# An extra pair's rows of x gathered through DRAM instead of by one-hot products

## The chip, the cores and the metric

The kernel runs on one core of one Trainium2 chip. The metric is the device time of one execution in microseconds, median of three runs. All times in the profile are in microseconds from the start of the span unless marked ns.

## The reference

Attention with random features gives x (1152 tokens of 512). A first mixture-of-experts layer sends each token to the one of eight experts with the highest logit; a second layer sends every token through four experts. Only the first of these two matters here:

```python
e_idx = np.argmax(x @ w_gate, axis=1)
for e in range(E):
    mask = e_idx == e
    if not mask.any():
        continue
    h = np.maximum(x[mask] @ w1[e], 0.0)
    ye = h @ w2[e]
    out[mask] = gate_w[mask, None] * eom[mask, e, None] * ye
```

## The kernel before

Tokens lie in four chunks of 288 (two batches of 576). Each chunk is made of two main tiles of 128 rows and a rest of 32; the four rests share one tile. Each batch has a main expert, the one that most of its tokens choose, and a chunk goes through it whole: `unit1` is layer 1 (96 products into tiles `ph`, whose results ACT and DVE turn into `hh` and `hl`), `unit2_blocks` is layer 2 in four blocks of 24 products (tiles `py`), each multiplied by a row of gates (`gate_row`, tiles `dg`, `pg`, `gb`) and written to `x2T`. The products are done in split precision, three for each (lines 645 to 647).

Pairs of a chunk and another expert that some of its tokens chose are extras. `extras` (line 985) finds them on DVE from the counts. One of them is treated apart: the first pair, where it has at most 32 tokens (`SLOTS`). All other extras go through a loop behind a branch (`tc.If(nx > 0)`, line 1189) whose lists of experts and chunks (`le_t`, `lc_t`, and the selector `mt`) `extras` makes too, with passes over 128x1024 elements (lines 1027 to 1040).

The pair taken apart goes as follows. Its expert and chunk are read into registers from `wi_t` (lines 1056, 1057). SP loads the expert's layer-1 weights raw (`xw1`, line 1138 reads them) and then three tiles `xt` of the chunk's rows of x from the DRAM copy `xs` (lines 1062, 1063). `picked` makes a mask of its tokens, two products `pr` (lines 1079, 1080) count them, and DVE turns that into `rank`, each token's slot (lines 1082 to 1085). `og` is the one-hot matrix of the slots (line 1089), `ogf` the same times the gates. The products `px` (line 1109) of `og` and `xt` gather up to 32 rows for each of the three tiles; ACT copies them to `xpart`, four transposes and a DVE sum (`turned_sum`, lines 1104, 1105) give `xg`, the gathered columns. Layer 1 is `phx` (line 1138), copied, turned and summed into `hx`; layer 2 is `yx` (line 1149, with the weights `xw2` in `own`, `w2x` and two more tiles of the tag `xt`); `pyf` folds it, `pa` (line 1168) spreads it back, and DVE adds it to `x2T` (line 1173). E1, the main expert of the second batch, has its layer-1 weights loaded behind that (`E1.load1`, line 116, into the two buffers that `xw1` leaves) with the register read from `le_t`, and its layer-2 weights only behind the branch (line 143, called from `E1.load2`).

On each engine the order of instructions is set when the program is built: a planner with estimated durations takes, whenever an engine comes free, the earliest statement of the program that it holds to be ready. So a later statement may stand before an earlier one (`px` of line 1109 stands among the products of a `unit2` block that the program begins after it, and a memset of line 1177 runs before `extras`). On the chip each engine then follows this order strictly: an instruction that waits holds up everything behind it on its engine. `pin` and `tc.issue_after` force an order by hand.

Of the kernel before, what the change touches and what calls it, by code (L numbers as in the profile page):

```python
# [9 lines left out]
F32 = mybir.dt.float32  # L10
F32R = mybir.dt.float32r
I32 = mybir.dt.int32
AF = mybir.ActivationFunctionType
ALU = mybir.AluOpType
# [8 lines left out]
DM = 512  # L23
NE, NE2, FF = 8, 4, 1024
KB, FB = DM // 128, FF // 128
# [5 lines left out]
SLOTS = 32  # L31
# [7 lines left out]
def moe_stack(ctx, tc, q, k, v, omega, w_gate, w_ogate, mw1, mw2, dprobs, dw1, dw2, out):  # L39
    nc = tc.nc  # L40
    TT, STT, TS = nc.vector.tensor_tensor, nc.vector.scalar_tensor_tensor, nc.vector.tensor_scalar
# [120 lines left out]
    ap = pool_a.enter_context(tc.tile_pool(name="ap", bufs=2))  # L162
# [5 lines left out]
    for c, w, pattern, base in ((0, 32, [[1, 32]], 0), (32, 32, [[1, 32]], 1), (64, 8, [[-1, 8]], 8),  # L168
# [3 lines left out]
                       pattern=pattern, base=base, channel_multiplier=0)  # L172
# [45 lines left out]
    def load_v(b, hh):  # L218
        raw["v", b, hh] = load_main(v, b, hh, "v", G, D + 1)

    xs = ctx.enter_context(tc.tile_pool(name="dp", bufs=1, space=bass.MemoryType.DRAM)).tile([9, 128, DM], F32, name="xs")
    om2 = cp.tile([128, 2, D], F32, name="om2")
    for r in range(2):
        nc.scalar.dma_start(om2[:, r, :], omega)
# [34 lines left out]
    def pin(i):  # L259

        k = i.ins.engine
        if k in last_of:
            tc.add_manual_dep(i.ins, last_of[k].name,
                              mybir.DependencyInfo(mybir.DependencyClass.NoSync, mybir.DependencyReason.DATA))
        last_of[k] = i.ins
        return i
# [399 lines left out]
    E0, kv_step = None, {}  # L666
# [36 lines left out]
    while st < n:  # L703
# [72 lines left out]
        if gate_at == st - 1:  # L776
            gate_late[0] = (0, lg) + main_expert(0, mx, eq, ps_t, "pt")
            E0 = main_weights(0, nc.gpsimd)
# [101 lines left out]
    nd2 = Turn((ps_n, "nd"), (ps_m, "nm"))  # L880
# [46 lines left out]
    RINGS = ((ps_t, "pt"), ND)  # L927

    def unit1(c, w1, *rings):
        xhc = [xh[:, kb, NC * c:NC * c + NC] for kb in range(KB)]  # L930
        xlc = [xl[:, kb, NC * c:NC * c + NC] for kb in range(KB)]
        return l1(w1, xhc, xlc, *(rings or RINGS))

    def unit2_blocks(c, w2, hs, late=None):
        gb = gate_row(sel_static(c, c // 2))
        for d in range(KB):
            if d == KB - 1 and late is not None:
                late += [l2_block(w2, hs, d, (ps_k, "kv")), gb]
                yield
                return  # L940
            y = l2_block(w2, hs, d, (ps_k, "kv") if (c, d) == (0, 0) else None)
            for dst, src in zip(x2cols(c), (slice(0, 256), slice(256, NC))):
                TT(x2T[:, d, dst], y[:, src], gb[:, src], op=ALU.mult)
            yield
# [8 lines left out]
    def x2cols(c):  # L953
        return slice(256 * c, 256 * c + 256), slice(1024 + 32 * c, 1056 + 32 * c)
# [18 lines left out]
    hs = first  # L973
# [8 lines left out]
    x2T = yp.tile([128, KB, NX], F32, tag="y", name="x2T")  # L982


    def extras():
        fl = cp.tile([128, 4, NE], F32, name="fl")
        TS(fl, cnt, 0.5, None, op0=ALU.is_gt)
        nb = cp.tile([128, 2, NE], F32, name="nb")
        TS(nb, ohb, -1.0, 1.0, op0=ALU.mult, op1=ALU.add)
        for c in range(4):  # L990
            TT(fl[:, c], fl[:, c], nb[:, c // 2], op=ALU.mult)
        flat = fl.rearrange("p c e -> p (c e)")
        pa = cp.tile([128, 32], F32, name="pa")
        pb_ = cp.tile([128, 32], F32, name="pb_")
        src = flat
        for i, sft in enumerate((1, 2, 4, 8, 16)):
            dst = (pa, pb_)[i % 2]
            nc.vector.tensor_copy(dst[:, 0:sft], src[:, 0:sft])
            TT(dst[:, sft:32], src[:, sft:32], src[:, 0:32 - sft], op=ALU.add)
            src = dst  # L1000

        sel = cp.tile([128, 32], F32, name="sel1")
        STT(sel, src, 1.0, flat, op0=ALU.is_equal, op1=ALU.mult)
        sc = cp.tile([128, 32], F32, name="sc")
        TT(sc, sel, cnt.rearrange("p c e -> p (c e)"), op=ALU.mult)
        few = cp.tile([128, 2], F32, name="few")
        nc.vector.tensor_reduce(few[:, 0:1], sc, axis=AX.X, op=ALU.add)
        TS(few[:, 0:1], few[:, 0:1], SLOTS + 0.5, None, op0=ALU.is_lt)
        TS(few[:, 1:2], src[:, 31:32], 0.5, None, op0=ALU.is_gt)
        TT(few[:, 0:1], few[:, 0:1], few[:, 1:2], op=ALU.mult)  # L1010
        TS(sel, sel, few[:, 0:1], None, op0=ALU.mult)
        TT(flat, flat, sel, op=ALU.subtract)
        TS(src, src, few[:, 0:1], None, op0=ALU.subtract)
        where = cp.tile([128, 2], F32, name="where")
        for i, tab in enumerate((ue, uc)):
            TT(sc, sel, tab.rearrange("p c e -> p (c e)"), op=ALU.mult)
            nc.vector.tensor_reduce(where[:, i:i + 1], sc, axis=AX.X, op=ALU.add)
        wi = cp.tile([128, 2], I32, name="wi")
        nc.vector.tensor_copy(wi, where)
        nx = cp.tile([128, 1], I32, name="nx")  # L1020
        nc.vector.tensor_copy(nx, src[:, 31:32])
        mine = cp.tile([128, 32], F32, name="mine")
        TS(mine, iota, src[:, 31:32], None, op0=ALU.is_equal)
        TT(src, src, flat, op=ALU.mult)
        mt = lp.tile([128, 32, 4, NE], F32, name="mt", bufs=1)
        mv = mt.rearrange("p i c e -> p i (c e)")
        TT(mv, src.unsqueeze(1).to_broadcast([128, 32, 32]), iota1.unsqueeze(2).to_broadcast([128, 32, 32]),
           op=ALU.is_equal)
        lists = []
        pool_t = ExitStack()  # L1030
        ltp = pool_t.enter_context(tc.tile_pool(name="ltp", bufs=1))
        for nm, tab in (("le", ue), ("lc", uc)):
            t = ltp.tile([128, 32, 32], F32, tag="lt", name="lt")
            TT(t, mv, tab.rearrange("p c e -> p (c e)").unsqueeze(1).to_broadcast([128, 32, 32]), op=ALU.mult)
            s = cp.tile([128, 32], F32, name=nm + "f")
            nc.vector.tensor_reduce(s, t, axis=AX.X, op=ALU.add)
            if nm == "le":
                STT(s, mine, ef[1][:, 0:1], s, op0=ALU.mult, op1=ALU.add)
            si = cp.tile([128, 32], I32, name=nm)
            nc.vector.tensor_copy(si, s)  # L1040
            lists.append(si)
        pool_t.close()
        return nx, mt, lists[0], lists[1], sel.rearrange("p (c e) -> p c e", c=4), wi

    blocks = unit2_blocks(0, E0.w2, hs)
    next(blocks)
# [2 lines left out]
    gate_count(1, *ND)  # L1049
    for _ in blocks:  # L1050
        pass
    nx_t, mt, le_t, lc_t, sel1, wi_t = extras()
    hs = unit1(1, E0.w1)
    pool_x = ExitStack()
    xg_ = pool_x.enter_context(tc.tile_pool(name="xg", bufs=1))
    ex = nc.values_load(wi_t[0:1, 0:1], engines=[SP], min_val=0, max_val=NE - 1)
    cx = nc.values_load(wi_t[0:1, 1:2], engines=[SP, DVE], min_val=0, max_val=3)
    X = Expert(dyn(mw1, ex), dyn(mw2, ex))
    xw1 = X.raw1()
    xt = [xg_.tile([128, DM], F32, tag="xt", name="xt", bufs=3) for _ in range(3)]  # L1060
    for t in range(2):
        nc.sync.dma_start(xt[t], xs[bass.ds(cx * 2 + t, 1)].rearrange("o p d -> (o p) d"))
    nc.sync.dma_start(xt[2], xs[8])

    def picked(nm, main, rest):

# [10 lines left out]
    mask, fac = picked("mask", f32(oh_all), f32(ohr)), picked("fac", g_all, grm)  # L1077
# [3 lines left out]
    rank = xg_.tile([128, 2, 3], F32, name="rank")  # L1081
    nc.vector.tensor_copy(rank, pr)
    for t in (1, 2):
        for i in range(t):
            TT(rank[:, 0, t:t + 1], rank[:, 0, t:t + 1], rank[:, 1, i:i + 1], op=ALU.add)
    og = xg_.tile([128, 3, SLOTS], F32, name="og")
    ogf = xg_.tile([128, 3, 4, SLOTS], F32, name="ogf")
    for t in range(3):
# [10 lines left out]
    def turned_sum(dst, src, n, bank):  # L1099

        pool, tag = bank
        ps = pool.tile([128, 4, n], F32, tag=tag, name="pts")
        for i in range(4):
            nc.tensor.transpose(ps[:, i], src[:, 128 * i:128 * i + 128], ident[:n, :n])
        nc.vector.tensor_reduce(dst, ps.rearrange("p i (k s) -> p i s k", s=SLOTS), axis=AX.X, op=ALU.add)

    px = nd2.tile([128, DM], F32, tag="nd", name="px")
    for t in range(3):
        nc.tensor.matmul(px[SLOTS * t:SLOTS * t + SLOTS], og[:, t], xt[t], start=True, stop=True)
    part = xg_.tile([128, 2, DM], F32, tag="part", name="xpart", bufs=1)  # L1110
    nc.scalar.copy(part[0:96, 0], px[0:96])
    xg = xg_.tile([128, KB, SLOTS], F32, name="xg")
    turned_sum(xg, part[0:96, 0], 96, RINGS[0])
    psx = ps_t.tile([128, 3, 128], F32, tag="pt", name="psx")
    for t in range(3):
        nc.tensor.transpose(psx[:, t], ogf[:, t].rearrange("p a s -> p (a s)"), ident)
# [4 lines left out]
    E1 = Expert(dyn(mw1, e), None, nc.vector)  # L1121
    xw2 = X.raw2(0, own)
    xw2 = [xw2[:, f] for f in range(4)]
    w2x = xg_.tile([128, 2, DM], F32, name="w2x")
    nc.sync.dma_start(w2x, X.wb[512:768, :].rearrange("(f p) d -> p f d", p=128))
    xw2 += [w2x[:, 0], w2x[:, 1]]
    for f in (6, 7):
# [44 lines left out]
        for dst, src in ((bass.ds(cx * 256, 256), slice(0, 256)), (slice(1024, NX), slice(256, 384))):  # L1172
            TT(x2T[:, d, dst], x2T[:, d, dst], pa[:, src], op=ALU.add)

    last = []
    for cols in x2cols(1):
        pin(nc.gpsimd.memset(x2T[:, KB - 1, cols], 0.0))
    blocks = unit2_blocks(1, E0.w2, hs, last)
    next(blocks)
    next(blocks)  # L1180
    yf = second()
    next(blocks)
# [304 lines left out]
```

## Time and profile before

| | us |
|---|---|
| median of 3 runs | 573.14 (572.75 to 573.24) |
| the profiled execution | 573.32 |
| its span, first to last instruction | 571.3 |
| PE busy in the span | 563.3 |
| DVE / ACT / POOL busy | 395.4 / 251.1 / 264.0 |

The profiled execution lies 0.18 us above the median and 2.0 us above its own span. The stretch that the change touches lies between 98 us (`extras`) and 153 us (the first layer-2 block of the third chunk). Only PE's row starts are exact enough to be subtracted from each other: the products of a full chunk follow each other every 0.133 us (12.8 us for 96), whatever durations their rows show.

### The profile page before, as it was taken

To read this page: it belongs to the slowest core of one execution; us is meant where nothing else is said; L and a number is where in the kernel's file an instruction comes from. 1 tells how busy PE (TensorE), PEld (TensorE's weight loads), DVE (VectorE), ACT (ScalarE), POOL (GpSimd) and SP (SyncE) were. 2 spreads that over 40 slices of the span, in tenths; PEclk is the share of its full clock that TensorE was granted. 3 is DMA by queue.
4 is the path that set the end of the run, shared out by engine and by line. 5 is a ranking of instruction groups with operands and counts; after the bars stand their busy time and mean duration, and the time that the engine had idled before them with its cause. 6 is when DMAs were issued, how large, how long until landed. Compare 5 with 4: busy or idle time off the path is not lost.

```text
span 571.3 us, 11664 instructions
## 1 busy us (share of the span) xinstructions
PE 563.3 (99%) x4526; PEld 510.5 (89%) x4527; DVE 395.4 (69%) x865; ACT 251.1 (44%) x622; POOL 264.0 (46%) x318
## 2 busy tenths in 40 slices
PE   8999999999999999999999999999999999999997
PEld 7787899987999999889989999899998999989996
DVE  7877978946679886666676666766666666665664
ACT  5988844135634434444342443334433344343230
POOL 5996464000010227673663836638456375563210
PEclk9999999999999999999999999999999999999999
DMA  8861560483600400220220022022022002000004
GB/s 181 211 167 39 176 207 1 168 294 110 224 1 3 136 11 2 75 74 1 75 73 1 2 75 74 2 73 75 1 74 75 0 28 85 38 2 1 0 1 165
DMA packets 42473, 42.83 MB, mean 75 GB/s; under 512 B 14896, under 2 KB 31792, under 8 KB 42416
## 3 DMA queue, kind: packets, MB, share of 16 engines
q1 hardware_dynamic: 42128, 42.00, 23.7%
q8 instruction: 36, 0.59, 0.4%
q14 instruction: 21, 0.17, 0.1%
q10 hardware_dynamic: 288, 0.07, 0.1%
HBM read 37.34 MB, written 4.72 MB: 74 GB/s over the span
## 4 chain that ended last, share of the span: by engine, by line
PE 73%; DMA 1%; DVE 1%; issue 0%; ACT 0%; SPq 0%; ACTq 0%
PE po L646 11%; PE po L645 11%; PE po L647 11%; PE pp L647 10%; PE pp L646 10%; PE pp L645 10%; PE py L645 2%; PE py L647 1%; PE py L646 1%; DMA st<-in_moe_w_dram 1%; PE ph L646 1%; PE ph L647 1%; PE ph L645 1%; DVE wlo L105 1%; DVE hl L641 0%
## 5 line engine op out<-in xcount | busy, mean ns | idle before, releaser
L105 POOL TENSOR_TENSOR wlo<-st,whi 128x512 fp32r<-128x512 f32 x96 | 115.7, 1226 | 178.6 <-ACT whi L104 72.0
L104 ACT CAST whi<-st 128x512 fp32r<-128x512 f32 x116 | 65.6, 590 | 117.4 <-PE po L647 49.3
L646 PE MATMUL po<-wlo,hh 128*128 128x512 f32 x290 | 112.8, 389 | 0.0
L645 PE MATMUL po<-whi,hh 128*128 128x512 f32 x290 | 112.7, 389 | 0.0
L647 PE MATMUL po<-whi,hl 128*128 128x512 f32 x290 | 112.4, 388 | 0.0
L888 POOL TENSOR_TENSOR hl<-c,hh 128x320 fp32r<-128x320 f32 (+1 forms) x64 | 52.2, 816 | 84.6 <-ACT hh L887 69.2
L647 PE MATMUL pp<-xh,wlo 128*128 128x320 f32 (+1 forms) x256 | 75.8, 296 | 0.0
L646 PE MATMUL pp<-xl,whi 128*128 128x320 f32 (+1 forms) x256 | 75.7, 296 | 0.0
L645 PE MATMUL pp<-xh,whi 128*128 128x320 f32 (+1 forms) x256 | 75.6, 295 | 0.0
L1422 DVE SCALAR_TENSOR_TENSOR oa<-po,pb,oa 128x512 f32<-128x512 f32 x75 | 55.1, 747 | 29.1 <-PE po L647 29.1
L647 PEld LDWEIGHTS po<-whi,hl 128*128 128x128 f32 x290 | 54.5, 188 | 11.4
L645 PEld LDWEIGHTS po<-whi,hh 128*128 128x128 f32 x290 | 54.5, 188 | 10.4
L646 PEld LDWEIGHTS po<-wlo,hh 128*128 128x128 f32 x290 | 54.5, 188 | 10.1
L1422 DVE SCALAR_TENSOR_TENSOR ob<-po,pb,ob 128x512 f32<-128x512 f32 x59 | 44.2, 749 | 26.8 <-PE po L647 26.8
L1377 DVE TENSOR_TENSOR c<-u,pp 128x320 f32<-128x320 f32 (+1 forms) x96 | 43.3, 453 | 22.4 <-PE pp L647 21.9
L886 ACT ACTIVATE c<-c 128x320 f32<-128x320 f32 (+1 forms) x64 | 28.5, 445 | 50.7 <-DVE c L1377 50.0
L646 PEld LDWEIGHTS pp<-xl,whi 128*128 128x128 f32 x256 | 48.5, 190 | 1.2
L645 PEld LDWEIGHTS pp<-xh,whi 128*128 128x128 f32 x256 | 48.5, 190 | 1.2
L647 PEld LDWEIGHTS pp<-xh,wlo 128*128 128x128 f32 x256 | 48.5, 190 | 0.0
L641 DVE SCALAR_TENSOR_TENSOR hl<-c,hh 128x320 fp32r<-128x320 f32 (+1 forms) x64 | 44.4, 725 | 0.5 <-ACT hh L640 0.2
L351 ACT ACTIVATE e<-pj,nb 128x128 f32<-128x128 f32 x144 | 39.1, 388 | 6.1 <-DVE nb L342 5.9
L645 PE MATMUL ph<-xh,whi 128*128 128x288 f32 x128 | 38.3, 299 | 0.5 <-PEq L1189 0.4
(280 smaller groups left out, 1249.7 us busy)
## 6 DMA issues: line engine op xcount, KB each, us to landing
st<-in_moe_w_dram SPq DMA_DIRECT2D x36, 512.0 KB, 4.5
st<-in_moe_w_dram SPq DMA_DIRECT2D x8, 1024.0 KB, 6.8
q<-in_q_dram SPq DMA_DIRECT2D x4, 512.0 KB, 4.9
v<-in_v_dram SPq DMA_DIRECT2D x16, 128.0 KB, 5.0
xs<-xn SPq DMA_DIRECT2D x16, 128.0 KB, 3.0
k<-in_k_dram SPq DMA_DIRECT2D x3, 512.0 KB, 5.1
out_dram<-oa SPq DMA_DIRECT2D x5, 256.0 KB, 2.0
own<-in_moe_w_dram SPq DMA_DIRECT2D x1, 1024.0 KB, 7.6
```

Of the source, the lines that this page charges most:

```text
L104: p(heng.tensor_copy(hi, src) if heng else nc.scalar.copy(hi, src))
L105: p(eng.tensor_tensor(lo, src, f32(hi), op=ALU.subtract))
L351: pin(nc.scalar.activation(e[:, i], st_p[u][a][:, i], AF.Exp, bias=nb[:, a, i:i + 1]))
L641: return lambda: p(STT(hl, src, 0.0, f32(hh), op0=ALU.max, op1=ALU.subtract))
L645: p(nc.tensor.matmul(ps, sh_, mh, start=start, stop=False))
L646: p(nc.tensor.matmul(ps, sh_, ml, start=False, stop=False))
L647: p(nc.tensor.matmul(ps, sl_, mh, start=False, stop=stop))
L886: nc.scalar.activation(c, c, AF.Relu)
L888: nc.gpsimd.tensor_tensor(hl, c, f32(hh), op=ALU.subtract)
L1377: TT(c, u, p, op=op)
L1422: STT(oacc[T], po, pc, oacc[T], op0=ALU.mult, op1=ALU.add)
```

## The change

The three one-hot products `px` and the copy `xpart` go. In their place each tile's masked rows are sent by an indirect transfer from POOL into a DRAM tile `xz` of 32 rows at the index `ix` (the rank; an index of 4096 and more, which the bounds check leaves out, for rows that aren't masked). The three `xz` are zeroed before, and read back after, by plain transfers from POOL into `xr`, whose transposes and sum give `xg` as before. The mask, the ranks and the transfers come ahead of `unit1(1)` in the program, the lists of the loop (`lists_of`) after `xg`, the first block of `unit2(1)` ahead of the transposes, and the loads of `xt` ahead of those of `xw1`.

```diff
@@ -218,7 +218,9 @@
-    xs = ctx.enter_context(tc.tile_pool(name="dp", bufs=1, space=bass.MemoryType.DRAM)).tile([9, 128, DM], F32, name="xs")
+    dp = ctx.enter_context(tc.tile_pool(name="dp", bufs=1, space=bass.MemoryType.DRAM))
+    xs = dp.tile([9, 128, DM], F32, name="xs")
+    xz = [dp.tile([SLOTS, DM], F32, name=f"xz{t}") for t in range(3)]
@@ -1019,6 +1021,9 @@
         nc.vector.tensor_copy(nx, src[:, 31:32])
+        return nx, sel.rearrange("p (c e) -> p c e", c=4), wi, src, flat
+
+    def lists_of(src, flat):
         mine = cp.tile([128, 32], F32, name="mine")
@@ -1027,10 +1032,8 @@
-        pool_t = ExitStack()
-        ltp = pool_t.enter_context(tc.tile_pool(name="ltp", bufs=1))
         for nm, tab in (("le", ue), ("lc", uc)):
-            t = ltp.tile([128, 32, 32], F32, tag="lt", name="lt")
+            t = xg_.tile([128, 32, 32], F32, tag="part", name="lt", bufs=1)
@@ -1039,8 +1042,7 @@
-        pool_t.close()
-        return nx, mt, lists[0], lists[1], sel.rearrange("p (c e) -> p c e", c=4), wi
+        return mt, lists[0], lists[1]
@@ -1049,18 +1051,25 @@
-    nx_t, mt, le_t, lc_t, sel1, wi_t = extras()
-    hs = unit1(1, E0.w1)
+    nx_t, sel1, wi_t, src_t, flat_t = extras()
     pool_x = ExitStack()
     xg_ = pool_x.enter_context(tc.tile_pool(name="xg", bufs=1))
     ...
-    xw1 = X.raw1()
     xt = [xg_.tile([128, DM], F32, tag="xt", name="xt", bufs=3) for _ in range(3)]
     for t in range(2):
         nc.sync.dma_start(xt[t], xs[bass.ds(cx * 2 + t, 1)].rearrange("o p d -> (o p) d"))
     nc.sync.dma_start(xt[2], xs[8])
+    xw1 = X.raw1()
+    w2x = xg_.tile([128, 2, DM], F32, name="w2x")
+    nc.gpsimd.memset(w2x[0:SLOTS, 0], 0.0)
+    pi = xg_.tile([128, 1], I32, name="pi")
+    nc.gpsimd.iota(pi, pattern=[[0, 1]], base=4096, channel_multiplier=1)
+    pf = xg_.tile([128, 1], F32, name="pf")
+    nc.gpsimd.tensor_copy(pf, pi)
+    for t in range(3):
+        nc.gpsimd.dma_start(xz[t], w2x[0:SLOTS, 0])
@@ -1083,6 +1092,19 @@
+    place = xg_.tile([128, 3], F32, name="place")
+    far = pf.to_broadcast([128, 3])
+    TT(place, rank[:, 0], far, op=ALU.subtract)
+    TT(place, place, mask, op=ALU.mult)
+    ix = xg_.tile([128, 3], I32, name="ix")
+    TT(ix, place, far, op=ALU.add)
+    for t in range(3):
+        nc.gpsimd.indirect_dma_start(xz[t], bass.IndirectOffsetOnAxis(ap=ix[:, t:t + 1], axis=0), xt[t], None,
+                                     bounds_check=SLOTS - 1, oob_is_err=False)
+    xr = xg_.tile([128, DM], F32, tag="xt", name="xr", bufs=3)
+    for t in range(3):
+        nc.gpsimd.dma_start(xr[SLOTS * t:SLOTS * t + SLOTS], xz[t])
+    hs = unit1(1, E0.w1)
@@ -1104,13 +1126,14 @@
-    px = nd2.tile([128, DM], F32, tag="nd", name="px")
-    for t in range(3):
-        nc.tensor.matmul(px[SLOTS * t:SLOTS * t + SLOTS], og[:, t], xt[t], start=True, stop=True)
-    part = xg_.tile([128, 2, DM], F32, tag="part", name="xpart", bufs=1)
-    nc.scalar.copy(part[0:96, 0], px[0:96])
+    last = []
+    for cols in x2cols(1):
+        pin(nc.gpsimd.memset(x2T[:, KB - 1, cols], 0.0))
+    blocks = unit2_blocks(1, E0.w2, hs, last)
+    next(blocks)
     xg = xg_.tile([128, KB, SLOTS], F32, name="xg")
-    turned_sum(xg, part[0:96, 0], 96, RINGS[0])
+    turned_sum(xg, xr[0:96], 96, RINGS[0])
+    mt, le_t, lc_t = lists_of(src_t, flat_t)
@@ -1121,7 +1144,6 @@
-    w2x = xg_.tile([128, 2, DM], F32, name="w2x")
     nc.sync.dma_start(w2x, X.wb[512:768, :].rearrange("(f p) d -> p f d", p=128))
@@ -1172,11 +1194,6 @@
-    last = []
-    for cols in x2cols(1):
-        pin(nc.gpsimd.memset(x2T[:, KB - 1, cols], 0.0))
-    blocks = unit2_blocks(1, E0.w2, hs, last)
-    next(blocks)
     next(blocks)
     yf = second()
```

## Rows read from the trace of the kernel before

**Rows 1.** The page's first part: busy time (share of the span) and instructions of each engine.

```profile
PE 563.3 (99%) x4526; PEld 510.5 (89%) x4527; DVE 395.4 (69%) x865; ACT 251.1 (44%) x622; POOL 264.0 (46%) x318
```

**Rows 2.** Busy time of each engine in stretches around the change, granted clock, DMA.

```profile
core 0: us, PE busy (x) PEld busy (x) DVE busy (x) ACT busy (x) POOL busy (x), PEclk, DMA share, GB/s
104.00:117.00 13.00, 13.00 (x100) 13.00 (x99) 9.66 (x26) 3.21 (x8) 0.00 (x0) 1.00 0.75 258
117.00:122.00 5.00, 5.00 (x35) 3.49 (x38) 3.28 (x16) 1.15 (x3) 0.00 (x0) 1.00 0.88 309
...
138.00:141.00 3.00, 2.55 (x19) 2.35 (x19) 0.98 (x3) 1.90 (x7) 0.00 (x0) 1.00 0.54 139
```

**Rows 3.** PE in order of time: start, us, line, operation, tile.

```profile
103.67 0.29 PE L645 MATMUL ph<-xh,whi 128*128 128x288 f32 x1
...
116.47 0.28 PE L1079 MATMUL pr<-mask,upper 128*128 128x3 f32 x2
...
116.83 0.38 PE L645 MATMUL py<-hh,whi 128*128 128x288 f32 x1
117.05 0.29 PE L646 MATMUL py<-hl,whi 128*128 128x288 f32 x1
...
117.97 0.30 PE L647 MATMUL py<-hh,wlo 128*128 128x288 f32 x1
118.20 1.41 PE L1109 MATMUL px<-xt,og 128*32 128x512 f32 x6
119.53 0.40 PE L645 MATMUL py<-hh,whi 128*128 128x288 f32 x1
...
120.44 0.49 PE L1104 MATMUL pts<-ident,xpart 96*128 96x96 f32 x4
...
121.58 1.92 PE L1138 MATMUL phx<-st,xg 128*32 128x512 f32 x16
...
124.62 0.51 PE L922 MATMUL pg<-dg,ones 128*128 128x288 f32 x2
124.97 0.29 PE L647 MATMUL py<-hh,wlo 128*128 128x288 f32 x1
```

**Rows 4.** The chain that ended last, in order of time: start, us, what.

```profile
137.99 7.48 DMA st<-in_moe_w_dram
...
152.62 0.53 PE pg L922 x2
```

**Rows 5.** DVE in order of time.

```profile
103.19 1.22 DVE L1027 TENSOR_TENSOR mt<-pa,consts 128x1024 f32<-128x1024 f32 x1
...
104.76 0.16 DVE L1019 CAST wi<-where 128x2 int32<-128x2 f32 x1
...
109.19 0.17 DVE L1040 CAST le<-lef 128x32 int32<-128x32 f32 x1
...
131.97 2.50 DVE L105 TENSOR_TENSOR wlo<-st,whi 128x512 fp32r<-128x512 f32 x4 [0.36 <-ACT whi L104]
134.70 0.52 DVE L943 TENSOR_TENSOR x2T<-py,gb 128x256 f32<-128x256 f32 x2 [0.23 <-PE py L647]
135.59 2.20 DVE L1173 TENSOR_TENSOR x2T<-x2T,pa 128x256 f32 x8 [0.37 <-issue]
```

**Rows 6.** SP's transfers in order of time: start, us of issue, line.

```profile
106.31 1.04 SPq L138 DMA_DIRECT2D st<-in_moe_w_dram  x2
110.97 0.93 SPq L1062 DMA_DIRECT2D xt<-xs  x2
...
122.71 1.24 SPq L116 DMA_DIRECT2D st<-in_moe_w_dram  x2
```

**Rows 7.** Transfers: line, engine, count, KB each, us to landing.

```profile
xt<-xs SPq DMA_DIRECT2D x3, 256.0 KB, 5.3
...
xs<-xn SPq DMA_DIRECT2D x4, 64.0 KB, 2.2
```

**Rows 8.** POOL in order of time.

```profile
156.34 2.73 POOL L105 TENSOR_TENSOR wlo<-st,whi 128x512 fp32r<-128x512 f32 x2 [64.23 <-PE py L647]
```

## The prediction

> **What bounds the kernel now.** I read the page's busy shares first: PE is busy for 563.3 of 571.3 us [rows 1], so a change counts for what it takes from PE's queue or makes PE wait. Then the stretches: from 104 to 122 us PE is busy throughout, at the full granted clock [rows 2], so there is no idle PE time to win there, only work to remove. Then PE in order of time. The 96 products of `unit1(1)` begin at 103.67 and end where `pr` begins, at 116.47: 12.8 us, 0.133 each. In the `unit2` block behind it stands `px`: after the product at 117.97 the next was due at 118.10 and comes at 119.53, so `px` costs PE 1.43 us [rows 3]. Last I read the chain that ended last. It doesn't follow PE here: it goes through the transfer of E1's layer-2 weights, issued at 137.99, and from there through ACT and DVE to PE at 152.62 [rows 4]. The transfer goes out when DVE has passed the branch, which it does after the eight additions of `pa` (135.59 for 2.20, so 137.79) [rows 5]. PE itself idles for 0.45 us around the branch [rows 2]. So two paths run level into 152 us, and a gain counts only as far as both move: PE's queue, and DVE's additions with the transfer behind them.
>
> **What the change removes.** `px`: 1.43 us of PE. ACT's copy of `px` goes too, but its place between 119.53 and the transposes at 120.44 was filled with `py` products [rows 3], so it is worth nothing.
>
> **What it moves on PE.** `pr` now falls among the products of `unit1(1)` and no longer at a border. A product after another kind of work is followed after 0.22 instead of 0.13 us (116.83 to 117.05) [rows 3], so the move costs 0.09. `pg` (0.35, from 124.62 to 124.97) stands before or inside the first block instead of later: nothing. Transposes, `phx`, `yx`, `pa` stay. Sum for PE: -1.43 + 0.09 = -1.34 us, if it never waits.
>
> **When PE wants `xr`.** The first block comes ahead of the transposes now. It ends at 103.67 + 12.8 + 0.36 for `pr` + 0.09 + 0.35 for `pg` + 24 x 0.133 + 0.09 = 120.5 us [rows 3]. There PE's queue is in fixed order: if `xr` isn't there, everything behind the transposes waits, `unit2` products included.
>
> **When `xr` comes.** `wi` was written at 104.76, behind the 1.22 us pass of `mt` [rows 5], which now comes later in the program; so about 103.5. From the end of `wi` (104.92) to SP's next transfer it was 1.39 us [rows 5, 6], so `xt` goes out from 104.9, three issues of 0.47 each (0.93 for two) [rows 6], the last at 105.8. Landing: 2.2 us for the 64 KB stores to `xs`, 5.3 for `xt` behind the 2 MB of `xw1` [rows 7]. The loads now go ahead of `xw1` on a quiet queue; I take 3.5: first at 108.4, last at 109.3. The ranks are no later: mask, `pr`, `rank` and the three operations for `place` and `ix` end by about 107, as their inputs are there by `wi` and small operations on DVE are of 0.16 us, as that of `wi` itself [rows 5].
>
> No row shows a transfer issued from POOL, nor an indirect one. For an issue I take bounds of 0.5 us (SP's, 0.52 for each of `xw1`) and 1.4 (the longest POOL work in these rows, 2.73 for two) [rows 6, 8], and 1.0 between. For a landing the bounds are again 2.2 and 5.3 [rows 7], and I take 3.0: the pieces are 64 KB or less, but the DMA engines are 75 to 88% busy from 104 to 122 us [rows 2]. Three indirect transfers are then issued by 108.4 + 3.0 = 111.4, landed at 114.4; the last read-back, issued by 115.4, lands at 118.4, 2.1 us ahead of 120.5. By the low bounds it is 104.9 + 2.2 + 3 x 0.5 + 2.2 + 0.5 + 2.2 = 113.5; by the high ones 104.9 + 5.3 + 3 x 1.4 + 5.3 + 1.4 + 5.3 = 126.4. So the slack is 2.1 us, within +7.0 and -5.9: hidden is likelier than not, and far from sure.
>
> The Trainium skill, page "DMA: Bandwidth & Descriptors", section "Anatomy of one DMA — SWDGE (gpsimd) path", gives a POOL transfer 2.0 us and its bytes at 436 GB/s, so an estimate of 2.15 us for 64 KB; two such landings in place of my two would have `xr` there at 116.7. No run here shows it yet.
>
> **What else moves.** The zeroing of `xz`, the memset, `pi` and `pf` are POOL's; POOL has nothing between its memsets of `x2T` and 156.34, 64.23 us of idle time [rows 8], and nothing queued behind the indirect transfers but the read-backs and the branch. On SP, `xw1` goes behind three `xt` issues (1.4 us) that start 1.4 us earlier: it goes out at 106.3 as before, and is first read at 121.58 [rows 3, 6]. `lists_of` stands after `xg` in the program, but its inputs are there from 103 us, and DVE is busy for only 9.66 of the 13 us from 104 to 117 with those passes in it [rows 2]; the planner takes what is ready, so I expect them where they were, `le` near 109 [rows 5], at no cost.
>
> **What DVE gives on.** The transposes come at 120.5 against 120.44, so `phx` and the two transfers of `E1.load1` that wait for it (122.71) stay where they are [rows 3, 6]. Then DVE's last four `wlo` (131.97 for 2.50), too, move little, at most by some 0.5 (an estimate) if ACT, which copies `ys` ahead of the casts for them, comes to that earlier. Behind them DVE has the last `x2T` product (0.52 at 134.70) and the additions [rows 5]. PE has `pa` ready 1.34 earlier, but DVE is free for the additions at about 134.0 to 134.5, plus 0.52: 134.5 to 135.0 against 135.59. So the second path gains 0.6 to 1.1 us, and the smaller of the two gains counts: I take 0.9.
>
> **Sum.** 573.32 - 0.9 = 572.4 for the profiled execution; it lies 0.18 above the median of the runs, so 572.2 for the median.
>
> **Rivals.** (1) *The gather comes late.* For it: six transfers on an engine that no row shows issuing any, two landings in DRAM in a row, beside the extra expert's weights. Each us after 120.5 costs PE one; from 121.8 the gain is gone, from about 122.7 the kernel is slower by over 0.2%. With both landings at 4.5, and 1.4 for each issue it is 104.9 + 3.5 + 4.2 + 4.5 + 1.4 + 4.5 = 123.0, and with `xt` at 5.3 124.8. With 124.2: 3.7 - 1.34 = 2.4 us slower, 575.5. A mechanism of this kind: POOL held up by DVE's long passes, 1.22 us each [rows 5], for its three indirect issues and the last read-back: 118.4 + 4 x 1.22 = 123.3. The Trainium skill, page "SBUF — State Buffer", sections "SBUF: two separate sides" and "Who interferes with whom", says that POOL can't write a transfer's descriptors while DVE runs in a two-port mode; but it names copies, casts and scalar operations for that, not products and sums. The casts here are of 0.16 and 0.17 us [rows 5], so I give this mechanism 0.03 of the rival's chance.
>
> (2) *The whole 1.34 comes through.* If DVE or ACT are put in another order (the additions ahead of the last `wlo`, or `ys` ahead of all of them), the second path moves as far as PE: 571.8.
>
> (3) *The lists aren't moved up*, so that the change does something else than it says. Then `le` is written three passes (3.7 us) and some 0.5 after `xg` (121.6), at 125.8; `E1.load1` goes out at 127.2 instead of 122.71, the last `wlo` end at 138.9 in place of 134.5, and the additions with the transfer behind them come some 3 us later: 576.
>
> **How the numbers follow.** Hidden gather with part of the gain, 0.42, of which 0.12 end over 0.2% (1.15 us, about what a measurement of this kernel can tell from no change). Rival 2: 0.24. Rival 1: 0.26, of which 0.06 arrive between 120.5 and 122.7 and leave no difference. Rival 3: 0.08. Faster 0.12 + 0.24 = 0.36, same 0.30 + 0.06 = 0.36, slower 0.20 + 0.08 = 0.28. The likeliest alone spans 572.0 to 572.6. The range goes down past rival 2 to 571.3 and up to 575.5, which leaves out the later half of rival 1 and rival 3.
>
> **What would show it.** Right: `px` and its 1.43 us gone; the transposes on `xr` at 120 to 121 us without a wait of PE; POOL's transfers between 108 and 116; `le` before 112; DVE's additions ending 0.6 to 1.1 us earlier, E1's layer-2 transfer at 137.1. Wrong: a wait of PE for the transfer of `xr`; POOL issues of over 1.4 us or landings of over 4; `E1.load1` after 124; or PE through the branch earlier and the products at 152.6 not.

## The result, and the profile after

The changed kernel takes 576.19 us (median of 6 runs, 575.08 to 577.50), the one before 572.95 beside it (6 runs): a ratio of 1.0059 [1.0046, 1.0073]. It is slower by 3.24 us, on the other side of the forecast and 0.7 us above the range. It went by rival 1, the gather that comes late.

All lines of this section are of the profiled execution after, the slowest of the six (577.50 us, a span of 575.7); the line numbers are those of the changed file. First PE in order of time (start, us, line, operation, tile; in brackets the idle time before it and what ended it). It answers to [rows 3]:

```profile
104.28 0.28 PE L1088 MATMUL pr<-mask,upper 128*128 128x3 f32 x2
...
104.64 0.38 PE L647 MATMUL ph<-xh,whi 128*128 128x288 f32 x1
...
117.53 0.43 PE L924 MATMUL pg<-dg,ones 128*128 128x288 f32 x2
117.79 0.29 PE L647 MATMUL py<-hh,whi 128*128 128x288 f32 x1
...
120.85 0.29 PE L649 MATMUL py<-hh,wlo 128*128 128x288 f32 x1
124.80 0.55 PE L1126 MATMUL pts<-ident,xr 96*128 96x96 f32 x4 [3.66 <-DMA xr<-xz]
...
125.96 0.44 PE L649 MATMUL py<-hh,wlo 128*128 128x288 f32 x1
126.20 0.44 PE L647 MATMUL py<-hh,whi 128*128 128x288 f32 x1
...
126.82 2.96 PE L1160 MATMUL phx<-st,xg 128*32 128x512 f32 x16
```

`px` is gone, the counts `pr` stand ahead of `ph`, and the first layer-2 block stands ahead of the transposes, as the change says. The block ends at 121.14, and there PE stands still for 3.66 us until the read-back `xr` has landed. That wait is the loss. What follows it is slow as well: products are 0.24 us apart in place of 0.133, and `phx` takes 2.96 us in place of 1.92. The stretches say why (columns as in [rows 2]):

```profile
104.00:117.00 13.00, 13.00 (x101) 13.00 (x99) 11.77 (x40) 2.88 (x7) 3.86 (x3) 1.00 0.76 257
117.00:121.00 4.00, 4.00 (x32) 3.90 (x30) 0.72 (x3) 0.70 (x2) 1.58 (x3) 1.00 1.01 336
121.00:125.00 4.00, 0.34 (x4) 0.20 (x3) 0.52 (x2) 0.00 (x0) 0.00 (x0) 1.00 0.42 132
125.00:129.00 4.00, 4.00 (x24) 2.13 (x26) 0.56 (x1) 0.66 (x2) 0.00 (x0) 0.57 0.00 0
```

PE's granted clock is 0.57 from 125 to 129 us, mostly the lower of its two levels (1.2 of 2.4 GHz), after the standstill from 121.14 to 124.80. The DMA engines are full (1.01) from 117 to 121, just when the gather's last transfers are under way, and have nothing left to do from 125 on.

POOL, which had no work here [rows 8], now issues the gather. Its zeroing of `xz` is issued by 85 us:

```profile
82.83 1.77 POOL L1072 DMA_DIRECT2D xz<-w2x  x3
...
109.52 1.71 POOL L1102 DMA_INDIRECT xz<-xt,ix  x1 [16.76 <-DMA xt<-xs]
111.53 1.18 POOL L1102 DMA_INDIRECT xz<-xt,ix  x1 [0.30 <-issue]
113.02 0.97 POOL L1102 DMA_INDIRECT xz<-xt,ix  x1 [0.30 <-issue]
117.69 1.23 POOL L1106 DMA_DIRECT2D xr<-xz  x2 [3.71 <-DMA xz<-xt,ix]
119.58 0.50 POOL L1106 DMA_DIRECT2D xr<-xz  x1 [0.66 <-DMA xz<-xt,ix]
```

The transfers issued from 100 to 130 us (count, KB each, median us from issue to landing), answering to [rows 7], and SP's queue, answering to [rows 6]:

```profile
own<-in_moe_w_dram SPq DMA_DIRECT2D x1, 1024.0 KB, 12.5
xt<-xs SPq DMA_DIRECT2D x3, 256.0 KB, 2.7
...
xr<-xz POOLq DMA_DIRECT2D x3, 64.0 KB, 5.4
xz<-xt,ix POOLq DMA_INDIRECT x3, 6.6
```

```profile
105.98 0.91 SPq L1062 DMA_DIRECT2D xt<-xs  x2
...
107.56 1.02 SPq L138 DMA_DIRECT2D st<-in_moe_w_dram  x2
108.78 0.37 SPq L143 DMA_DIRECT2D own<-in_moe_w_dram  x1
...
128.81 1.42 SPq L116 DMA_DIRECT2D st<-in_moe_w_dram  x2
```

`xt` lands quickly, ahead of the weights. The three scatters and the three read-backs come behind 2 MB of `xw1` and 1 MB of `own`, and land in 6.6 and 5.4 us. DVE, answering to [rows 5]:

```profile
104.22 0.15 DVE L1021 CAST wi<-where 128x2 int32<-128x2 f32 x1
...
115.52 0.17 DVE L1043 CAST le<-lef 128x32 int32<-128x32 f32 x1
...
141.47 2.19 DVE L1195 TENSOR_TENSOR x2T<-x2T,pa 128x256 f32 x8
```

**How the times are compared below.** The same work before the change's stretch ends at 103.67 us in the kernel before, at 104.28 after, at 105.49 in the first experiment: that much differs between executions. So PE's rows are counted from the first product after the first chunk's last layer-2 block (us; each is a row's start less those times; the last column is the span's end):

```
                          pts     phx      yx      pa  ph of chunk 3   its pg     end
before                  16.77   17.91   25.12   30.92          35.69    48.95  467.63
after                   20.52   22.54   29.06   34.86          39.63    52.34  471.42
without the scatters    16.70   18.11   23.60   29.39          34.23    46.95  465.61
later weights held      16.82   18.29   23.77   34.71          39.49    52.63  471.73
two blocks ahead        20.96   22.43   26.97   32.83          38.04    53.28  472.45
the wait filled         20.93   22.14   27.88   33.70          38.47    51.19  470.53
one landing, one `pw`   17.15   18.51   24.12   29.91          34.68    47.39  465.66
```

### The profile page after: what moved, and what is told of

It is laid out like the page before. It is cut to its first block, busy times and chain, and to the rows that moved or that the text cites. A ratio compares the mean times of both kernels' runs of the same rounds, so it can differ in the third digit from the quotient of the medians.

```text
span 575.7 us, 11684 instructions
## 1 busy us (share of the span) xinstructions
PE 563.5 (98%) x4520; PEld 511.2 (89%) x4521; DVE 394.5 (69%) x868; ACT 250.2 (43%) x621; POOL 271.8 (47%) x330
## 4 chain that ended last, share of the span: by engine, by line
PE 74%; DVE 0%; issue 0%
PE po L647 11%; PE po L648 11%; PE po L649 11%; PE pp L649 10%; PE pp L647 10%; PE pp L648 10%; PE ph L647 2%; PE py L647 1%; PE py L649 1%; PE ph L649 1%; PE ph L648 1%; PE py L648 1%; PE pg L924 0%; DVE ob L1456 0%
## 6 DMA issues: line engine op xcount, KB each, us to landing
own<-in_moe_w_dram SPq DMA_DIRECT2D x1, 1024.0 KB, 12.5
```

## The experiments

Three questions had to be told apart: whether the wait for the gather is the whole loss or the moves cost something too; what makes the gather late (POOL's issues, the two landings in a row, or the weights beside them); and whether the wait can be covered or the chain has to be shortened.

**The moves without the gather.** The three indirect transfers are left out, everything else stays, so the extra pair's gathered rows are zeros: that part of the result is missing.

```diff
-    for t in range(3):
-        nc.gpsimd.indirect_dma_start(xz[t], bass.IndirectOffsetOnAxis(ap=ix[:, t:t + 1], axis=0), xt[t], None,
-                                     bounds_check=SLOTS - 1, oob_is_err=False)
```

> The changed kernel without its three indirect transfers: the zeroed tiles are read straight back, so the extra pair's rows count as zeros (that part of the result is left out), and everything else stands as in the changed kernel. Late gather (the time is lost in the 3.66 us that PE waits for xr, and in the granted clock of 0.57 from 125 to 129 us behind that wait): the wait is gone, the clock stays at 1.00, and 1.0 to 1.4 us of the kernel before are saved, 571.6 to 572.0. Rival, the moves cost by themselves (lists, load order, first block ahead): no wait of PE, and still 573.5 or more.

Measured: 571.53 us (6 runs), 0.9968 [0.9956, 0.9980]. PE doesn't wait for `xr`, and the granted clock is 1.00 throughout. POOL, the transfers from 100 to 130 us, and PE of this kernel:

```profile
110.32 1.52 POOL L1103 DMA_DIRECT2D xr<-xz  x3 [16.41 <-DMA xt<-xs]
```

```profile
xr<-xz POOLq DMA_DIRECT2D x3, 64.0 KB, 6.4
```

```profile
122.19 0.50 PE L1123 MATMUL pts<-ident,xr 96*128 96x96 f32 x4
```

So all that the change takes from PE comes through, some 1.6 us, and everything from there to 576.19, 4.66 us, comes with the scatters. One landing is hidden with ease even at 6.4 us: `xr` is there by about 118 (110.32, 1.52 for the issues, 6.4), the transposes follow at 122.19.

**The moves alone, `px` kept.** Mask, ranks and the loads of `xt` go where the change puts them, the lists behind the ranks; `px`, its copy and the place of the first block are as before.

```diff
...
-    for t in range(3):
-        nc.gpsimd.dma_start(xr[SLOTS * t:SLOTS * t + SLOTS], xz[t])
...
+    px = nd2.tile([128, DM], F32, tag="nd", name="px")
+    for t in range(3):
+        nc.tensor.matmul(px[SLOTS * t:SLOTS * t + SLOTS], og[:, t], xt[t], start=True, stop=True)
```

> The changed kernel's moves without its gather: mask and ranks ahead of unit1(1), xt loaded ahead of xw1, lists behind the ranks, but px and its copy as before, and the first unit2 block behind the transposes as before. Late gather: the moves are worth nothing either way, within 0.8 us of the kernel before, 572.2 to 573.8. Rival, the moves cost by themselves: 575 or more, with the loss in a wait behind the lists or behind the weights.

Measured: 572.99 us (11 runs), 0.9993 [0.9984, 1.0002]. The moves are worth nothing either way. Between this kernel and the last one lie `px` and its copy, the read-backs and the place of the first block: 572.99 - 571.53 = 1.46 us, beside the 1.43 of the prediction for `px`.

**The later weights held back.** `own`, `w2x` and the two layer-2 loads behind it wait for `xr` by way of a small POOL copy from it into each; `xw1` stays in front.

```diff
+    nc.gpsimd.tensor_copy(own[0:96, 0:1], xr[0:96, 0:1])
     xw2 = X.raw2(0, own)
...
+    nc.gpsimd.tensor_copy(w2x[0:96, 0, 0:1], xr[0:96, 0:1])
     nc.sync.dma_start(w2x, X.wb[512:768, :].rearrange("(f p) d -> p f d", p=128))
...
+        nc.gpsimd.tensor_copy(xw2[f][0:96, 0:1], xr[0:96, 0:1])
         nc.sync.dma_start(xw2[f], X.wb[128 * f:128 * f + 128, :])
```

> The changed kernel with the loads of own and w2x (2 MB of the extra expert's layer-2 weights) held back until xr has landed, by a small copy on POOL from xr into each of them. Landings are long because they share the DMA engines with weights: xw1 still beside the scatters, nothing beside the read-back, so the scatters land in 4 to 5 us and the read-back in 2.5 to 3, xr is there at about 119 to 120, and PE's wait for it falls under 0.5 us (yx may wait for its weights instead). Rival, the transfers are slow by themselves (indirect, issued from POOL, through DRAM): landings of 6 and 5 us and a wait of over 3 us as in the changed kernel.

Measured: 576.73 us (4 runs), 1.0054 [1.0038, 1.0069]. Its transfers from 100 to 130 us, and PE's longest wait (what waits, for what, us in total, times, longest):

```profile
xr<-xz POOLq DMA_DIRECT2D x3, 64.0 KB, 2.1
xz<-xt,ix POOLq DMA_INDIRECT x3, 6.3
```

```profile
PE pyf L1182 <- ACT ys L1179: 3.1, 1, 3.1
```

The read-back lands in 2.1 us in place of 5.4, `xr` is there just as PE comes to the transposes (120.59), without a wait. The scatters, with `xw1` still beside them, take 6.3 (6.6 in the changed kernel), not the 4 to 5 expected. The time isn't better, as a wait of 3.1 us stands later instead. It is hardly for the weights held back: `yx` begins 23.77 us after the common point (23.60 without the scatters), and its second half takes 1.56 us in place of 1.04. The 3.1 us are a wait for ACT's copy `ys`, and ACT has the casts of E1's layer-1 weights ahead of it in its order. Those weights now go out right behind the held loads, and land after 8.0 and 11.0 us in place of 5.1 and 7.5 without the scatters. ACT, and the stretch from 133 us:

```profile
132.02 2.18 ACT L104 CAST whi<-st 128x512 fp32r<-128x512 f32 x4 [5.49 <-DMA st<-in_moe_w_dram]
134.10 0.57 ACT L1179 COPY ys<-yx 128x512 f32<-128x512 f32 x1
```

```profile
133.00:137.00 4.00, 2.27 (x16) 2.07 (x17) 2.79 (x6) 3.23 (x8) 0.00 (x0) 0.77 0.16 58
```

Behind this wait, too, the granted clock is low (0.77), though the gather was on time.

**All weights held back.** The same, with `xw1` behind `xr` too (one execution).

```diff
-    xw1 = X.raw1()
...
+    xw1 = [stp.tile([128, KB, 512], F32, tag="st", name="st") for _ in range(2)]
+    for g in range(2):
+        nc.gpsimd.tensor_copy(xw1[g][0:96, 0, 0:1], xr[0:96, 0:1])
+        nc.sync.dma_start(xw1[g], X.wa[:, 512 * g:512 * g + 512].rearrange("(k p) f -> p k f", p=128))
```

> As the run with own and w2x held back, but xw1 is held back until xr has landed too, so nothing else moves beside the scatters. If sharing with weights is what makes landings long, the scatters land in 2.5 to 3.5 us instead of 6.3, the read-back in 2.1, and xr is there 3 to 4 us earlier, some 13 us after the end of the first chunk's products; phx and yx then wait for their weights. Rival, an indirect transfer of 128 rows takes 6 us by itself: landings as in that run.

Measured: 583.78 us. The transfers from 100 to 130 us:

```profile
xr<-xz POOLq DMA_DIRECT2D x3, 64.0 KB, 2.1
xz<-xt,ix POOLq DMA_INDIRECT x3, 3.0
```

With nothing beside them the scatters land in 3.0 us and the read-backs in 2.1; POOL's issues are as long as ever (1.82, 1.19, 0.99), and yet `xr` is there by 117.59, 13.39 us after the common point; in the changed kernel it comes after 20.52. So the weights beside them make the landings long. They can't be held back in this way, as PE then waits for them: 2.5 us in `phx` and 3.9 at the branch.

**More cover.** Two blocks of `unit2` ahead of the transposes in place of one.

```diff
     blocks = unit2_blocks(1, E0.w2, hs, last)
     next(blocks)
+    next(blocks)
     xg = xg_.tile([128, KB, SLOTS], F32, name="xg")
...
-    next(blocks)
     yf = second()
```

> The changed kernel with two unit2 blocks instead of one ahead of the transposes of xr (48 products behind pg instead of 24), so PE comes to them 3.2 us later, at 20.0 us after the end of the first chunk's products instead of 16.8. Late gather, and only the wait counts: the wait falls from 3.7 to about 0.5 us, the clock stays at 1.00, PE is through the branch 1 us earlier than before, about 572. Rival, the chain behind xg is then too late in its turn (fewer products are left to stand beside phx, hx, yx, pa, and E1.load1 goes out 2 to 3 us later than before): the time comes back as waits of PE ahead of pa or behind the branch, 573.5 to 575.

Measured: 577.02 us (4 runs), 1.0064 [1.0049, 1.0080]. PE's waits from 103 to 155 us:

```profile
PE ph L647 <- DVEq L1206: 3.2, 1, 3.2
PE pts L1126 <- DMA xr<-xz: 0.9, 1, 0.9
```

The wait for `xr` falls from 3.66 to 0.9 us, and 3.2 us appear at the branch: the wait that the rival expected. The branch waits for DVE's additions, and these stand behind the last `wlo`:

```profile
136.45 2.50 DVE L105 TENSOR_TENSOR wlo<-st,whi 128x512 fp32r<-128x512 f32 x4 [0.97 <-ACT whi L104]
...
139.30 2.19 DVE L1196 TENSOR_TENSOR x2T<-x2T,pa 128x256 f32 x8
```

So the work from `xr` to the branch hangs together as a chain: `phx`; E1's layer-1 weights, loaded into the buffers that `phx` frees, with `yx` beside them; ACT's casts and copies; `wlo`; the additions. `pa` itself begins at 136.48, and isn't what DVE waits for. The block that covers the beginning of this chain is missing at its end. So the loss goes with the time at which `xr` comes; the wait only changes its place. The clock, expected at 1.00, falls again, this time behind the wait at the branch:

```profile
141.00:145.00 4.00, 3.31 (x14) 3.34 (x15) 2.41 (x6) 1.26 (x1) 0.00 (x0) 0.50 0.48 161
```

At the branch this kernel is 1.6 us ahead of the changed one (38.04 against 39.63). From there to `pg` it takes 15.24 us in place of 12.71, and so it ends behind it.

**The wait filled.** Sixteen products of `ones` by `ones`, whose results nobody uses, stand where PE waits. They keep PE at work, and don't make `xr` earlier.

```diff
+    fill = ps_t.tile([128, 128], F32, tag="pt", name="fill")
+    for _ in range(16):
+        nc.tensor.matmul(fill, ones, ones, start=True, stop=True)
     turned_sum(xg, xr[0:96], 96, RINGS[0])
```

> The changed kernel with 16 products of ones (some 3 us, results unused) in PE's queue between the first unit2 block and the transposes, that is in the time in which PE waits for xr. If the loss is the wait plus the low granted clock behind it, the clock stays at 1.00, the rest of the wait is under 1 us and the time falls by what the clock had taken, 1.2 to 1.7 us of the changed kernel's slower runs: 574.5 to 575. Rival, the products after the wait are slow for another reason (their operands, the DMA traffic): phx takes 2.9 us again and the time stays at 576.

Measured: 576.00 us (5 runs), 1.0046 [1.0033, 1.0060]. Its stretch behind the transposes, and `phx`:

```profile
125.00:129.00 4.00, 3.90 (x33) 2.22 (x34) 0.70 (x2) 1.65 (x3) 0.00 (x0) 1.00 0.04 12
```

```profile
126.31 1.92 PE L1163 MATMUL phx<-st,xg 128*32 128x512 f32 x16
```

The clock stays at 1.00 and `phx` takes 1.92 us again: it was the standstill that lowered the clock, not the gather, as the two kernels above with a standstill elsewhere show as well. In the profiled executions `pa` follows the transposes after 12.77 us in place of 14.34, 1.57 less, of which 0.41 are lost as the transposes come later, and the kernel's end comes 0.9 earlier. In the medians only 0.2 of it is left, within the intervals, and the expected 574.5 to 575 is missed. How much the clock bears in the median stays open.

**One landing in place of two.** The masked rows' numbers, not the rows, go through the one-hot matrix: three products `pw` of one column give each slot its row in `xs`, and a single indirect transfer fetches the 32 rows straight into `xr`. `xt`'s loads, `xz`, its zeroing and the read-backs go.

```diff
...
+    STT(vf[:, 0:2], where[:, 1:2].to_broadcast([128, 2]), 256.0, vf[:, 0:2], op0=ALU.mult, op1=ALU.add)
+    pw = nd2.tile([SLOTS, 1], F32, tag="nd", name="pw")
+    for t in range(3):
+        nc.tensor.matmul(pw, og[:, t], vf[:, t:t + 1], start=t == 0, stop=t == 2)
+    ix = xg_.tile([SLOTS, 1], I32, name="ix")
+    nc.vector.tensor_copy(ix, pw)
+    xr = xg_.tile([128, DM], F32, tag="xt", name="xr", bufs=3)
+    nc.gpsimd.indirect_dma_start(xr[0:SLOTS], None, xs.rearrange("t p d -> (t p) d"),
+                                 bass.IndirectOffsetOnAxis(ap=ix[:, 0:1], axis=0), bounds_check=1151, oob_is_err=False)
...
```

> One transfer instead of six: the one-hot matrix og times a column of row numbers (three products of one column) gives each slot's row in xs, and one indirect transfer reads the 32 rows from xs straight into xr; xt, the zeroing and the scatters are gone. Late gather: one issue of 1 to 1.7 us from about 108 and one landing of 3 to 7 us put xr at 112 to 117, ahead of PE's 121; no wait, and about 1.0 us of the kernel before saved (1.43 for px less some 0.4 for the three small products), 571.5 to 572.3. Rival, the moves cost by themselves: 573.5 or more without a wait.

Measured: 572.07 us (11 runs), 0.9982 [0.9973, 0.9991]. PE doesn't wait for `xr`. The three products cost it 1.04 us, most of what `px` had cost. So they went next:

**The same with one product.** DVE sums the row numbers over the three tiles first (the lines that differ from the kernel just shown).

```diff
+    row = xg_.tile([128, SLOTS], F32, name="row")
+    TS(row, og[:, 0], vf[:, 0:1], None, op0=ALU.mult)
+    for t in (1, 2):
+        STT(row, og[:, t], vf[:, t:t + 1], row, op0=ALU.mult, op1=ALU.add)
     pw = nd2.tile([SLOTS, 1], F32, tag="nd", name="pw")
-    for t in range(3):
-        nc.tensor.matmul(pw, og[:, t], vf[:, t:t + 1], start=t == 0, stop=t == 2)
+    nc.tensor.matmul(pw, row, ones[:, 0:1], start=True, stop=True)
```

> The one-hop gather with its row numbers summed on DVE first (three small operations), so that one product of one column takes the place of three scattered among unit1's. The three cost PE 1.04 us between pr and pg against the kernel without scatters; one costs about 0.35. So 0.7 us under the first one-hop kernel, 571.2 to 571.7, 1.4 to 1.8 us under the kernel before. Rival, the time isn't bound there (the transfer of E1's layer-2 weights is): no better than 572.1.

Measured: 571.34 us (6 runs), 0.9968 [0.9956, 0.9981]: faster than both kernels, by 1.6 and 4.9 us. POOL, the transfers from 100 to 130 us, and PE:

```profile
108.72 1.14 POOL L1102 DMA_INDIRECT xr<-xs,ix  x1 [16.16 <-DVE pa L1028]
```

```profile
xr<-xs,ix POOLq DMA_INDIRECT x1, 5.7
```

```profile
121.29 0.43 PE L1119 MATMUL pts<-ident,xr 32*128 32x32 f32 x4
```

The landing is as long beside the weights as any other (5.7 us), but it is one: `xr` is there at 114.4, 6.9 us ahead of the transposes.

## Why the prediction was wrong

**The step that failed is "When `xr` comes".** The path was set out rightly, and every part of it is in the trace; its terms were too small, the landings above all. Forecast 118.4, measured 124.80, 6.4 us later, term by term:

- `xt` goes out at 105.98, not 104.9: +1.1, of which 0.6 are the later start of this execution. From there to POOL's first scatter (109.52) it is 3.54 us; 3.5 was forecast.
- POOL's issues take 1.71, 1.18 and 0.97 us with 0.30 between them. The third begins 3.50 us after the first, not 2.0: +1.5.
- From the start of the third scatter (113.02) to the read-back that it releases (119.58) it is 6.56 us, not 1.0 + 3.0: +2.6.
- From there to PE (124.80) it is 5.22 us, not 4.0: +1.2.

The bounds, 113.5 to 126.4, held the time; the value taken between them didn't. Even the bounds held by an error: the rows count a landing from the start of its issue, and the prediction added the last issue of each hop to it once more. By its own terms, counted once, `xr` was due at 116.4, within 112.5 and 123.6, and so even the late bound lies ahead of what came (124.2 with the later start taken off).

For a landing I took 3.0, near the 2.2 of the small stores, because the pieces are small. The row to take was the other one: `xt`'s 5.3 behind `xw1` [rows 7], since it had the same neighbour in the queues; the scatters' 6.6 lie above even that. The runs that hold the weights back settle it: 2.1 and 3.0 us without them, 5.4 and 6.6 with them. With all of them held back, `xr` came 13.39 us after the common point, ahead of the forecast (118.4 - 103.67 = 14.7), though POOL's issues were as long as ever. Of this, the scatters' part belongs to `xw1` (it stays at 6.3 when only the later loads are held) and the read-backs' to `own` and `w2x`. These came earlier by the change itself: `own` stood behind `xt` in SP's queue and went out at 113.17 before, at 108.78 after. The prediction followed `xw1` past the three issues of `xt`, and not `own`.

The Trainium skill, page "DMA: Bandwidth & Descriptors", section "Anatomy of one DMA — SWDGE (gpsimd) path", gave an estimate of 2.15 us for 64 KB. The trace agrees where next to nothing else runs (2.1 in both kernels that hold the later weights back), and doesn't beside the loads (5.4, and 6.4 without the scatters).

**When PE wants `xr`:** 120.5 forecast, 121.14 measured, 0.6 later as is the whole execution. Right, and so the slack was counted from the right end.

**The price of rival 1** was each us after the slot less 1.34: 3.66 - 1.34 = 2.3, or 575.5. The two executions after whose mean granted clock was 1.0 took 575.08 and 575.48; the four at 0.997, the profiled one among them, took 575.75 to 577.50. So the wait was priced rightly, and what a standstill does to the clock was not priced at all. The profiled execution shows it at about 1.6 us, from the transposes to `yx`: 8.54 in place of 6.90 in the kernel without scatters. For the median, the run with the filled wait leaves it between 0.2 and that. This is also what lies above the range.

**Its chance,** 0.26 in all, was too small by the prediction's own numbers: with the landing of the row that had the weights beside it the slack was gone.

**DVE as what holds POOL up** (a chance of 0.03, priced at 4 x 1.22 us) isn't borne out: DVE runs a pass of 1.22 us from 109.05 and another from 110.62, and POOL idles only 0.30 us between the scatters. Whether the first scatter's 1.71 holds some of it wasn't tried; at most it is part of the 1.5 us of the issues.

**PE's sum,** -1.43 + 0.09, was right to about 0.1 us: without the scatters PE comes to the third chunk 1.46 us earlier than before (34.23 against 35.69).

**"What DVE gives on" was right, and what follows it was not.** I let only 0.9 of 1.34 through, as E1's layer-2 weights go out behind DVE's additions. Without the scatters the whole came through, and a little more (1.64 us against the kernel before beside it; rival 2's result, 571.5 beside its 571.8). But not by rival 2's mechanism: the last `wlo` still stand ahead of the additions, and the first of the two transfers goes out 33.66 us after the common point against 34.32, 0.66 earlier, within the forecast 0.6 to 1.1. DVE in the kernel without scatters, and SP:

```profile
133.91 2.50 DVE L105 TENSOR_TENSOR wlo<-st,whi 128x512 fp32r<-128x512 f32 x4 [0.89 <-ACT whi L104]
136.75 2.20 DVE L1192 TENSOR_TENSOR x2T<-x2T,pa 128x256 f32 x8
```

```profile
139.15 1.14 SPq L143 DMA_DIRECT2D st<-in_moe_w_dram  x2
```

The kernel before had a loss behind that transfer, where I saw an equal path. PE in it, then in the kernel without scatters:

```profile
139.36 0.37 PE L645 MATMUL ph<-xh,whi 128*128 128x288 f32 x1 [0.45 <-PEq L1189]
...
152.62 0.53 PE L922 MATMUL pg<-dg,ones 128*128 128x288 f32 x2
```

```profile
139.72 0.37 PE L647 MATMUL ph<-xh,whi 128*128 128x288 f32 x1 [0.51 <-PEq L1203]
...
152.44 0.43 PE L924 MATMUL pg<-dg,ones 128*128 128x288 f32 x2
```

From the branch to `pg` it is 13.26 us there and 12.72 here, and here PE is bound by nothing but its own queue. So 0.54 us were lost on the chain through the transfer [rows 4] in that execution. The landing, which the prediction took as given, decided it: the two transfers took 7.5 and 9.4 us there and 5.2 and 7.1 here, so that the first was there 3.0 us earlier, 0.66 by its place behind DVE and 2.3 by its landing. Had it landed as before, `pg` could have come some 0.66 earlier (an estimate); it came 2.00 earlier. Why it lands faster wasn't tried.

**The lists** were expected near 109; `le` is written at 115.52. The planner did take them up, out of the program's order, so rival 3 doesn't hold; but their passes went behind the small operations of mask and ranks. It costs nothing: `E1.load1` waits for `phx`, and goes out 19.24 us after the common point without the scatters, 19.04 before.

## What to carry to other kernels

Take a transfer's landing from the row that had the same neighbours in the queues, not from the one of the same size: here 64 KB took 2.1 us alone and 5.4 to 6.4 beside weights, and a gather of two hops paid that twice. Where a late operand heads a chain that runs to the next common point, moving more work ahead of it only moves the wait (3.66 us there, 0.9 + 3.2 elsewhere); what helps is fewer hops, as row numbers sent through the product and one transfer for the rows. A standstill of PE is to be priced with its clock: in addition to the 3.66 us, products behind it ran 0.24 us apart in place of 0.133, and so they did behind the waits of 3.1 and 3.2 us in two of the experiments.

## What the runs showed of the hardware that was not expected

The scatters are slow without moving much. The profile's queue section counts 432 packets and 0.40 MB on POOL's queue after, 192 packets and 0.39 MB in the kernel without scatters: 240 packets for about 0.01 MB (a difference of rounded figures), in 6.6 us beside the weights and 3.0 without them. An indirect transfer holds POOL for 1.71, 1.18 and 0.97 us (128 indices each) or 1.14 (32 rows), a plain one of 64 KB for about 0.5. And a 1 MB load issued 0.74 us ahead of the scatters, `own`, took 12.5 us, against 7.6 in the kernel before; in the kernel without scatters it took 12.7, so the scatters don't make it slow. In every run that issues it within 2 us behind `xw1` it took 9.2 us or more; that this place is the cause wasn't tried by itself.
